# An mLSTM cell and a routed two-layer expert network on one core: weight copies on VectorE, clears on GpSimd, second-layer weights eight rows to a partition, first-layer weight columns at stride eight

## The chip, the core and the metric

The kernel runs on one core of one Trainium2 chip. The metric is the device time of one execution in microseconds, as the median over several runs; less is better. Engine names are those of the profile: PE is the matrix engine and PEld its weight loads, DVE is VectorE, ACT is ScalarE, POOL is GpSimd and SP is SyncE; a q behind a name (POOLq, SPq) is that engine's sequencer, which issues DMAs and waits.

## What is computed

Stage one is a recurrent cell over 4 batches, 8 heads, 768 steps and head width 40. Stage two sends each of the 3072 resulting rows of 320 numbers to one of 8 experts.

```python
# stage one, for t in range(768), per batch and head
m_new  = max(f + m, i);  fs = exp(f + m - m_new);  is_ = exp(i - m_new)
C = fs * C + is_ * outer(v, k);   n = fs * n + is_ * k
y = sigmoid(o) * (C @ q) / max(abs(n . q), 1)
# stage two, on x = y as 3072 rows of 320
logits = x @ w_gate                       # 320 x 8
e      = argmax(logits);  g = softmax(logits)[e]
out    = g * (relu(x @ w1[e]) @ w2[e])    # w1: 320 x 1024, w2: 1024 x 320, per expert
```

## The kernel before

**Stage one** works on 24 chunks of 128 steps, one chunk per turn `s` of a loop, all 8 heads at once. A turn loads q, k, v and the gate of chunk `s + 6` from SP's queue (L316), transposes q and k (L341), multiplies queries with keys (L359, L360) under a causal mask, carries the state (L379, L387), normalises the rows (L411 to L417) and, every second turn, computes the gate logits of two chunks (L447), the chosen experts and the places of the rows. `rank` (L506) counts with matmuls, `place` (L521) writes the slot of each row. `keep_rows` (L539, ACT) scales the rows and turns them to bf16, and `send` (L546, POOL) scatters 128 rows by slot into `x_sorted` in DRAM. Before that, `clear` writes zeros over the first 384 rows of each expert's part of `x_sorted` (L555, SP's queue, eight DMAs). PE runs a few matmuls whose product is overwritten (L354) beside the real ones, in turns 1 to 7 and in the last three.

**Stage two** is cut into groups of one or two tiles of 128 rows. I write (e, 0) for expert e's first two tiles and (e, 1) for its third tile; six "extra" tiles of whatever expert has rows left over come last. The first two groups, called `first` (0, 0) and `second` (1, 0), are written out by hand at the end of stage one. For the others a list `order` sets the sequence: (2,0), (0,1), (3,0), (1,1), (4,0), (2,1), (5,0), (3,1), (6,0), (4,1), (7,0), (5,1), (6,1), (7,1), then the six extras. The code fixes the order of all instructions by hand; no scheduler moves them. Each group does

- `turn`: transpose the rows (L233) and copy them out of PSUM on DVE (L234);
- `layer1`: 8 blocks of 128 hidden columns, three matmuls each (L245), the weights being the stationary operand; then a relu on DVE (L251) or ACT (L253);
- the `turn` of the group that follows;
- `layer2`: eight matmuls per tile (L258), a copy on ACT (L263), and a scatter of the tile to the output from POOL (L265).

The weights come from DRAM as float32 and are turned to bf16 by the DMAs themselves, all issued from POOL: two for an expert's first-layer weights (`weights_in`, L178; the first takes rows 0 to 255, the second rows 256 to 319) and one for its second layer (`weights_out`, L185). All experts' first-layer weights share one tile `w1_all` [128, 3, 8, 1024], all second-layer weights one tile `w2_all` [128, 8, 8, 320]. `weights_in(e + 2)` and `weights_out(e + 2)` stand in the code ahead of `layer1` of group (e, 0) for e = 2 to 5; those of experts 0 to 3 stand at the end of stage one. The framework puts a semaphore wait wherever an instruction reads or writes what another one wrote or read, as far as it can tell from their access patterns.

An extra tile learns its expert only from a register. For it `fetch` copies that expert's two weight matrices into buffers of their own (wx, 4 sets), with two DMAs from SP's queue (L736, L737), four groups ahead of use. `extras` (L675 to L703) is a run of small DVE instructions that works out these experts and rows, ahead of the third group of the list.

Of the kernel before, what the change touches and what calls it, by code (L numbers as in the profile page):

```python
# [19 lines left out]
def kernel(  # L20
# [41 lines left out]
    NJ = 3  # L62
# [2 lines left out]
    XU = 6  # L65
    NE = 2
    PE_ = 7
    XW = 4
    NV = 6
    NS = N + 128  # L70

# [14 lines left out]
    def pads(i):  # L86
        for t in (kp[i], qp[i]):
            nc.vector.memset(t[:, :, D:], 0.0)
        nc.vector.memset(v1[i][:, :, D:], 1.0)
# [93 lines left out]
    def weights_out(e0, n):  # L183
        e = slice(e0, e0 + n)
        nc.gpsimd.dma_start(  # L185
            w2_all[:, e].rearrange("p e a d -> p (e a) d"), moe_w2[e].rearrange("e (a p) d -> p (e a) d", p=128),
        )

    def apart(ins, group):
# [46 lines left out]
    def layer1(g, u):  # L236
        n = g["n"]
        per = 4 // n
        if u == 0:
            g["h"] = spot("h", [128, FB, n * 128], BF16)  # L240
        hp = spot("hp", [128, per, n * 128], F32)
        for i in range(per):
            fb = u * per + i
            for db in range(DB):
                nc.tensor.matmul(  # L245
                    hp[:, i, :], lhsT=g["w"][0][:, db, fb * 128 : (fb + 1) * 128], rhs=g["xT"][:, db, :],
                    start=(i == 0 and db == 0), stop=(db == DB - 1), skip_group_check=True,
                )
        dst = g["h"][:, u * per : (u + 1) * per, :]
        if u % 2 == 0:  # L250
            nc.vector.tensor_relu(dst, hp)  # L251
        else:
            nc.scalar.activation(dst, hp, AF.Relu)  # L253
# [26 lines left out]
    with tc.tile_pool(name="ring", bufs=1) as ring_pool, \  # L280
# [67 lines left out]
        def scores(s):  # L348
            d = st[s]
            kb, qb = d["kb"], d["qb"]  # L350
            sA = ps1.tile([128, PR, 128], F32, name="sA")
            sB = ps1.tile([128, PR, 128], F32, name="sB")
            for _ in range(3 if 1 <= s < 8 else 2 if s > NT - 4 else 0):
                nc.tensor.matmul(  # L354
                    sA[:].rearrange("p j t -> p (j t)"), lhsT=ident_b[:],
                    rhs=st[s - 1]["dA"][:].rearrange("p j t -> p (j t)"), start=True, stop=True,
                )
            for j in range(PR):
                nc.tensor.matmul(sA[:, j, :], lhsT=kb[0:D, j, :], rhs=qb[0:D, j, :], start=True, stop=True)  # L359
                nc.tensor.matmul(  # L360
                    sB[:, j, :], lhsT=kb[DP : DP + D, j, :], rhs=qb[DP : DP + D, j, :], start=True, stop=True,
                )
            d["dA"] = chk.tile([128, PR, 128], BF16, name="dA")
            nc.vector.tensor_tensor(d["dA"][:], sA[:], cmask[:, None, :].to_broadcast([128, PR, 128]), op=ALU.mult)
            d["dB"] = chk.tile([128, PR, 128], BF16, name="dB")
            nc.scalar.copy(d["dB"][:], sB[:])  # L366
            nc.gpsimd.affine_select(
                d["dB"][:], d["dB"][:], compare_op=ALU.is_ge, fill=0.0,
                base=0, pattern=[[0, PR], [1, 128]], channel_multiplier=-1,
            )  # L370
# [170 lines left out]
            )  # L541

        def send(t):
            if t >= NT - 7:
                nc.gpsimd.memset(tick[:], 0.0)
            ins = nc.gpsimd.indirect_dma_start(  # L546
                out=xs[:, :], out_offset=bass.IndirectOffsetOnAxis(ap=slots[:, t : t + 1], axis=0),
                in_=x_all[:, t, :], in_offset=None,
            )
            apart(ins, "rows_in")  # L550
            if t > 2 * PE_ + 1:
                tc.declare_no_dep(getattr(ins, "ins", ins), group="early", reason="later rows lie behind the early tiles")

        def clear(e):
            nc.sync.dma_start(xs[e * NS : e * NS + CAP, :].rearrange("(p j) d -> p (j d)", j=NJ), zrow[:])  # L555

        def do(f, i, *a):
            if 0 <= i < NT:
                f(i, *a)
# [10 lines left out]
            load(i)  # L570
        for i in range(1, NV):
            pads(i)
        for s in range(-3, NT):
            P, odd = (s - 4) // 2, s % 2
            last = s == NT - 1
            do(scores, s + 1)
            do(transposes, s + 2)
            if s == -3:
                masks()
            if s == -2:  # L580
                gates()
                router()
            do(values, s + 2)
            if s == NT - 3:
                weights_in(0, 1)
            if 0 <= s < E:
                nc.vector.memset(w1_all[:64, DB - 1, s, :], 0.0)
            pair = not odd and 0 <= P
            if pair:
                gate(P)  # L590
            do(states, s)
            do(load, s + 6 if s >= -1 else -1)
            if -1 <= s < 3:
                clear(2 * s + 2)
                clear(2 * s + 3)
            if pair:
                rank(P, s - 1)
            do(xtrans, s - 1)
            do(ogate, s + 2)
            do(attend, s)  # L600
            if pair:
                place(P)
                if P == PE_:
                    even_out(s - 1)
            do(keep_rows, s - 4)
            do(rows, s)
            if odd and 0 <= (s - 3) // 2:
                logits((s - 3) // 2, s - 1)
                choose((s - 3) // 2)
                count((s - 3) // 2)  # L610
            do(send, s - 5)
            late_consts(s + 1)
            if s == 20:
                for e in range(E):
                    receive(e, 0)
            if s == NT - 3:
                weights_out(0, 1)
            if s == NT - 2:
                weights_in(1, 1)
        weights_out(1, 1)  # L620
        send(NT - 5)
        gate(P0)
        rank(P0, NT - 1)
        place(P0)
        early = [dict(e=e, n=NE, k=0, si=0) for e in range(2)]
        spots.update(
            hp=[("sA", ps1), ("sB", ps1)], zp=[("tk", ps1), ("tq", ps1)], tp=[("dC", ps1)],
# [6 lines left out]
        first, second = early  # L634
        targets(0, 0)
        turn(first)
        for t in (NT - 4, NT - 3):
            keep_rows(t)
            send(t)
        for u in range(4):  # L640
            layer1(first, u)
        weights_in(2, 1)
        weights_out(2, 1)
        xtrans(NT - 1)
        targets(1, 0)
        turn(second)
        layer2(first, 0)
        logits(P0 + 1, NT)
        choose(P0 + 1)
        gate(P0 + 1)  # L650
        layer2(first, 1)
        layer1(second, 0)
        rank(P0 + 1, NT, 2 * E)
# [3 lines left out]
        for t in (NT - 2, NT - 1):  # L657
            keep_rows(t)
            send(t)
        for u in range(2, 4):  # L660
            layer1(second, u)
        weights_in(3, 1)
        weights_out(3, 1)
        layer2(second, 0)
        layer2(second, 1)

# [66 lines left out]
    def fetch(ex):  # L733
        wx1 = wk_pool.tile([128, DB, F], BF16, name="wx1", bufs=XW)
        wx2 = wk_pool.tile([128, FB, Dm], BF16, name="wx2", bufs=XW)
        nc.sync.dma_start(wx1[:], w1_all[:, :, bass.ds(ex, 1), :].rearrange("p a e b -> p a (e b)"))  # L736
        nc.sync.dma_start(wx2[:].rearrange("p a b -> p (a b)"), w2_all[:, bass.ds(ex, 1)].rearrange("p e a b -> p (e a b)"))  # L737
        return wx1, wx2

    def expert_of(x):  # L740
        return nc.sync.value_load(xe[0:1, bass.ds(x, 1)], min_val=0, max_val=E - 1)

    def row_of(x):
        return nc.sync.value_load(xb[0:1, bass.ds(x, 1)], min_val=0, max_val=E * NS - 128)
# [1 line left out]
    nc.vector.tensor_tensor(inv[:, :, NE:], posB[:], tot[:].unsqueeze(2), op=ALU.is_ge)  # L746
    for e in range(E):
        receive(e, 1)
    order = [(2, 0), (0, 1)]
    for e in range(3, E):  # L750
        order += [(e, 0), (e - 2, 1)]
    order += [(E - 2, 1), (E - 1, 1)]
    groups = [
        dict(e=e, n=(NE, NJ - NE)[k], k=k, si=(0, NE)[k], w=(w1_all[:, :, e, :], w2_all[:, e])) for e, k in order
    ] + [dict(n=1, x=x) for x in range(XU)]
# [1 line left out]
    def ready(g):  # L757
        if "x" in g:
            aim(g)
        else:  # L760
            targets(g["e"], g["k"])
        turn(g)

    ready(groups[0])
    for i, g in enumerate(groups):
        nw = g.get("e", E) + 2
        if i == 2:
            extras()
            for e_ in range(E):
                blank(e_)  # L770
        if i == 4:
            for x in range(XU):
                collect(groups[len(order) + x], row_of(x), invx[:, x : x + 1])
            exs = [expert_of(x) for x in range(XU)]
        x = i - len(order) + XW
        if 0 <= x < XU:
            groups[len(order) + x]["w"] = fetch(exs[x])
        if g.get("k") == 0 and nw < E:
            weights_in(nw, 1)
            weights_out(nw, 1)  # L780
        for u in range(FB * g["n"] // 4):
            layer1(g, u)
        if i + 1 < len(groups):
            ready(groups[i + 1])
        for j in range(g["n"]):
            layer2(g, j)
    one_order.close()
# [42 lines left out]
```

## Time and profile before

| | before |
|---|---|
| median of 3 runs (lowest, highest) | 222.78 us (222.73, 223.47) |
| the profiled execution: own time, span | 230.12 us, 228.4 us |
| PE busy, PEld busy | 200.0 us (88%), 171.6 us (75%) |
| DVE, ACT, POOL busy | 131.2, 119.0, 124.1 us |
| mean granted PE clock | 0.915 |
| weight DMAs of an expert (KB written, us to landing, median) | 512 KB 8.7; 128 KB 8.0; 640 KB 12.9 |
| copies for an extra tile | 768 KB 8.8; 640 KB 7.1 |

The page splits the span into 40 slices of 5.7 us. Stage one ends near 127 us and stage two fills the rest. "Idle before, releaser" in the groups is the time an engine stood still ahead of these instructions and what ended it. Times of single instructions are from one execution, so small differences are within what one execution shows.

### The profile page before, as it was taken

The page shows a single profiled execution, that of the slowest core. Times are in us where ns is not written, and L with a number is a line of the kernel's source. Part 1 is how long each engine was busy: PE and PEld are TensorE (multiplying, and loading weights), DVE is VectorE, ACT ScalarE, POOL GpSimd, SP SyncE. Part 2 cuts the span into 40 slices and gives each one's busy share as a digit, 9 for nine tenths or more (in the row PEclk, how much of TensorE's full clock was granted, in tenths as well). Part 3 has the DMA queues.
Part 4 walks back from the last instruction along what each step waited for, and adds up shares of the span by engine and source line. Part 5 has one row for each costly group of instructions (what it writes and reads, how often), then busy time and mean ns, then how long its engine had stood idle before and what let it go on. Part 6 is the DMA issues. An engine that isn't in the chain of part 4 may idle for free.

```text
span 228.4 us, 5745 instructions
## 1 busy us (share of the span) xinstructions
PE 200.0 (88%) x2049; PEld 171.6 (75%) x2049; DVE 131.2 (57%) x421; ACT 119.0 (52%) x275; POOL 124.1 (54%) x194
## 2 busy tenths in 40 slices
PE   2299999899999999989999699439699999999990
PEld 1168888689999999979999487327488888777770
DVE  7658878755458888888774533304834353333330
ACT  3457758744668988896943246203243433433330
POOL 5045584185166686677597855823557734333331
PEclk9999999955599999999985599958999999999999
DMA  7999999999989999898059999999999999999930
GB/s 134 174 189 167 214 199 205 203 177 192 163 151 176 169 174 188 146 193 158 17 100 284 228 232 182 174 222 234 212 216 225 216 235 311 401 399 372 392 115 0
DMA packets 122796, 46.47 MB, mean 203 GB/s; under 512 B 102474, under 2 KB 115917, under 8 KB 122768
## 3 DMA queue, kind: packets, MB, share of 16 engines
q1 hardware_dynamic: 108576, 29.50, 59.0%
q0 software_dynamic: 13728, 16.40, 36.6%
q8 instruction: 16, 0.26, 0.5%
q10 hardware_dynamic: 464, 0.21, 0.4%
q14 instruction: 12, 0.10, 0.1%
HBM read 39.38 MB, written 9.53 MB: 214 GB/s over the span
## 4 chain that ended last, share of the span: by engine, by line
PE 55%; DMA 18%; issue 7%; DVE 6%; POOL 5%; ACT 5%; SPq 3%; POOLq 0%; ACTq 0%
PE hp L447 7%; PE hp L379 7%; PE zp L258 6%; PE dC L387 6%; PE hp L245 5%; PE tk L341 5%; DMA w_all<-in_moe_w_dram 5%; PE tq L341 4%; PE xt L424 4%; DMA wx<-w_all 4%; PE sA L359 3%; POOL out_dram L265 3%; DMA x_all<-x_sorted 3%; PE sA L354 2%; DMA kq<-in_k_dram 2%
## 5 line engine op out<-in xcount | busy, mean ns | idle before, releaser
L251 DVE TENSOR_SCALAR h<-hp 128x512 bf16<-128x512 f32 x26 | 17.9, 690 | 38.7 <-PE hp L245 38.7
L265 POOL DMA_INDIRECT out_dram<-zo,s_idx x20 | 20.0, 1002 | 30.6 <-ACT zo L263 26.1
L245 PEld LDWEIGHTS <-w_all 128*128 128x128 bf16 x384 | 30.7, 100 | 6.0 <-issue 2.2
L417 POOL TENSOR_TENSOR x_sb<-x_sb,den 128x320 f32<-128x320 f32 x23 | 16.9, 733 | 27.5 <-DVE den L415 27.5
L546 POOL DMA_INDIRECT x_sorted<-x_all,slots x24 | 25.0, 1043 | 9.1 <-DMA kq<-in_q_dram 4.7
L245 PE MATMUL hp<-xT,w_all 128*128 128x128 bf16 (+1 forms) x336 | 28.9, 242 | 0.9 <-DVE xT L234 0.8
L253 ACT ACTIVATE h<-hp 128x512 bf16<-128x512 f32 x26 | 15.5, 597 | 24.5 <-PE hp L245 24.5
L258 PEld LDWEIGHTS <-h 128*128 128x128 bf16 x208 | 18.4, 101 | 12.7 <-DVE h L251 4.1
L258 PE MATMUL zp<-w_all,h 128*128 128x320 bf16 x160 | 25.8, 312 | 1.9 <-DMA out_dram<-zo,s_idx 1.9
L263 ACT COPY zo<-zp 128x320 f32<-128x320 f32 x26 | 11.1, 426 | 29.1 <-PE zp L258 27.5
L379 PE MATMUL hp<-C_sb,qT 104*128 104x82 f32 x160 | 23.3, 294 | 0.0
L379 PEld LDWEIGHTS hp<-C_sb,qT 104*128 104x128 f32 x160 | 22.3, 215 | 0.1
L341 PE MATMUL tk<-ident,kq 128*104 128x128 f32 x96 | 17.4, 310 | 5.4 <-DMA kq<-in_k_dram 5.4
L366 ACT CAST dB<-sB 128x512 bf16<-128x512 f32 x24 | 14.0, 584 | 12.9 <-PE sB L360 10.1
L426 ACT COPY xT<-xt 128x384 f32<-128x384 f32 x24 | 11.6, 483 | 16.9 <-PE xt L424 16.8
L447 PE MATMUL hp<-wg_sb,xT 128*128 128x8 f32 x144 | 20.2, 273 | 0.0
L387 PE MATMUL dC<-vA,kq 128*104 128x82 f32 x160 | 19.8, 272 | 0.0
L447 PEld LDWEIGHTS hp<-wg_sb,xT 128*128 128x128 f32 x144 | 19.5, 215 | 0.0
L329 POOL CAST vAb<-vA 128x328 bf16<-128x328 f32 x24 | 11.0, 457 | 13.5 <-DVE vA L327 13.5
L387 PEld LDWEIGHTS dC<-vA,kq 128*104 128x104 f32 x160 | 18.2, 188 | 0.0
L327 DVE TENSOR_TENSOR vA<-v,G_T 128x328 f32<-128x328 f32 x24 | 17.3, 722 | 0.7 <-DMA v<-in_v_dram 0.7
L341 PE MATMUL tq<-ident,kq 128*104 128x128 f32 x96 | 16.7, 303 | 0.2 <-DMA kq<-in_q_dram 0.2
(147 smaller groups left out, 432.4 us busy)
## 6 DMA issues: line engine op xcount, KB each, us to landing
w_all<-in_moe_w_dram POOLq DMA_DIRECT2D x8, 640.0 KB, 12.9
wx<-w_all SPq DMA_DIRECT2D x6, 768.0 KB, 8.8
w_all<-in_moe_w_dram POOLq DMA_DIRECT2D x8, 512.0 KB, 8.7
kq<-in_k_dram SPq DMA_DIRECT2D x24, 160.0 KB, 3.8
kq<-in_q_dram SPq DMA_DIRECT2D x24, 160.0 KB, 4.4
v<-in_v_dram SPq DMA_DIRECT2D x24, 160.0 KB, 4.1
o_sb<-in_o_gate_dram SPq DMA_DIRECT2D x24, 160.0 KB, 4.0
wx<-w_all SPq DMA_DIRECT2D x6, 640.0 KB, 7.1
```

The costliest lines, as they stand in the source:

```text
L245: nc.tensor.matmul(hp[:, i, :], lhsT=g["w"][0][:, db, fb * 128 : (fb + 1) * 128], rhs=g["xT"][:, db, :], start=(i == 0 and db == 0), stop= ...
L251: nc.vector.tensor_relu(dst, hp)
L253: nc.scalar.activation(dst, hp, AF.Relu)
L258: nc.tensor.matmul(zp, lhsT=g["h"][:, fb, j * 128 : (j + 1) * 128], rhs=g["w"][1][:, fb, :], start=(fb == 0), stop=(fb == FB - 1),)
L265: ins = nc.gpsimd.indirect_dma_start(out=out[:, :], out_offset=bass.IndirectOffsetOnAxis(ap=at, axis=0), in_=zo, in_offset=None, bounds_ch ...
L327: nc.vector.tensor_tensor(d["vA"][:], d["v"][:], Gb.unsqueeze(2).to_broadcast([128, H, D1]), op=ALU.mult)
L341: nc.tensor.transpose(tp[:, j, :], two(d[n], j), ident[:])
L379: nc.tensor.matmul(hp[:, 2 * j * D1 : (2 * j + 2) * D1], lhsT=d["qT"][:, j, :], rhs=st["C"][:, j].rearrange("p h d -> p (h d)"), start=(j ...
L387: nc.tensor.matmul(st["dC"][:, j], lhsT=two(d["k"], j), rhs=d["vA"][:, 2 * j : 2 * j + 2, :], start=(c == 0 and j == 0), stop=True, skip_g ...
L417: eng.tensor_tensor(x3d, x3d, den[:].unsqueeze(2).to_broadcast([128, H, D]), op=ALU.mult)
L447: nc.tensor.matmul(lg[:, i * E : (i + 1) * E], lhsT=st[t]["xT"][:, db * 128 : (db + 1) * 128], rhs=wg_sb[:, db, :], start=(fresh and i == ...
L546: ins = nc.gpsimd.indirect_dma_start(out=xs[:, :], out_offset=bass.IndirectOffsetOnAxis(ap=slots[:, t : t + 1], axis=0), in_=x_all[:, t, : ...
```

## The change

1. `weights_out` puts eight consecutive rows of w2 on a partition instead of every 128th row. Row r of the hidden layer then lies on partition r // 8, and so `layer1` takes the columns fb, fb + 8, fb + 16, ... for its block fb, a stride of eight elements.
2. `fetch` copies with two DVE instructions instead of two DMAs from SP. The register is loaded on DVE, the buffers are 3 sets instead of 4, and the call stands behind `ready` of the following group, two groups ahead of use.
3. `clear` is issued from POOL, one expert per turn in turns 0 to 7, instead of from SP, two per turn in turns -1 to 2.
4. `send` always has a one-row memset ahead of it; the first send comes in turn 9 instead of 5, after the clears, and they catch up, two in odd turns. The receives of the experts' first two tiles stand one turn earlier (19 instead of 20).
5. At the seam between the stages: three instead of two spare matmuls in the last three turns and six more ahead of `layer1` of `first`; gate, rank and place of the second last pair of chunks behind two of its four `layer1` steps; `weights_in(3)` and `weights_out(3)` ahead of `layer1(second, 2)` instead of behind `layer1(second, 3)`.
6. `order` is (2,0), (3,0), (0,1), (1,1), (4,0), (2,1), (5,0), (3,1), (4,1), (6,0), (5,1), (7,0), (6,1), (7,1).

```diff
-    XW = 4
+    XW = 3
...
-            w2_all[:, e].rearrange("p e a d -> p (e a) d"), moe_w2[e].rearrange("e (a p) d -> p (e a) d", p=128),
+            w2_all[:, e].rearrange("p e a d -> p e (a d)"), moe_w2[e].rearrange("e (p a) d -> p e (a d)", p=128),
...
-                    hp[:, i, :], lhsT=g["w"][0][:, db, fb * 128 : (fb + 1) * 128], rhs=g["xT"][:, db, :],
+                    hp[:, i, :], lhsT=g["w"][0][:, db, fb::FB], rhs=g["xT"][:, db, :],
...
-            for _ in range(3 if 1 <= s < 8 else 2 if s > NT - 4 else 0):
+            for _ in range(3 if 1 <= s < 8 or s > NT - 4 else 0):
...
-            if t >= NT - 7:
-                nc.gpsimd.memset(tick[:], 0.0)
+            nc.gpsimd.memset(tick[:], 0.0)
...
-            nc.sync.dma_start(xs[e * NS : e * NS + CAP, :].rearrange("(p j) d -> p (j d)", j=NJ), zrow[:])
+            nc.gpsimd.dma_start(xs[e * NS : e * NS + CAP, :].rearrange("(p j) d -> p (j d)", j=NJ), zrow[:])
...
-            if -1 <= s < 3:
-                clear(2 * s + 2)
-                clear(2 * s + 3)
...
-            do(send, s - 5)
+            upto = s - 4 if s >= 2 * PE_ + 4 else s - 5
+            for t in range(sent, min(upto + 1, sent + 1 + odd) if s > E else sent):
+                send(t)
+                sent = t + 1
...
+            if 0 <= s < E:
+                clear(s)
...
+        for _ in range(6):
+            j = ps1.tile([128, 512], F32, name="junk", tag="tk")
+            nc.tensor.matmul(
+                j[:], lhsT=ident_b[:], rhs=st[NT - 1]["dA"][:].rearrange("p j t -> p (j t)"), start=True, stop=True,
+            )
+        layer1(first, 0)
+        layer1(first, 1)
+        gate(P0)
+        rank(P0, NT - 1)
+        place(P0)
+        layer1(first, 2)
...
+        weights_in(3, 1)
+        weights_out(3, 1)
         for u in range(2, 4):
             layer1(second, u)
-        weights_in(3, 1)
-        weights_out(3, 1)
...
-        nc.sync.dma_start(wx1[:], w1_all[:, :, bass.ds(ex, 1), :].rearrange("p a e b -> p a (e b)"))
-        nc.sync.dma_start(wx2[:].rearrange("p a b -> p (a b)"), w2_all[:, bass.ds(ex, 1)].rearrange("p e a b -> p (e a b)"))
+        nc.vector.tensor_copy(wx1[:], w1_all[:, :, bass.ds(ex, 1), :].rearrange("p a e b -> p a (e b)"))
+        nc.vector.tensor_copy(wx2[:].rearrange("p a b -> p (a b)"), w2_all[:, bass.ds(ex, 1)].rearrange("p e a b -> p (e a b)"))
...
-    order = [(2, 0), (0, 1)]
-    for e in range(3, E):
-        order += [(e, 0), (e - 2, 1)]
-    order += [(E - 2, 1), (E - 1, 1)]
+    order = [(2, 0), (3, 0), (0, 1), (1, 1), (4, 0), (2, 1), (5, 0), (3, 1), (4, 1), (6, 0), (5, 1), (7, 0), (6, 1), (7, 1)]
...
-            exs = [expert_of(x) for x in range(XU)]
-        x = i - len(order) + XW
-        if 0 <= x < XU:
-            groups[len(order) + x]["w"] = fetch(exs[x])
...
             ready(groups[i + 1])
+        x = i - len(order) + XW - 1
+        if 0 <= x < XU:
+            groups[len(order) + x]["w"] = fetch(expert_of(x))
```

More of the change, by code (lines that the diff above doesn't have):

```diff
@@ L572 @@
             pads(i)
+        sent = 0
         for s in range(-3, NT):
@@ L604 @@
                     even_out(s - 1)
-            do(keep_rows, s - 4)
+            if s == 2 * PE_ + 4:
+                keep_rows(s - 4)
+                keep_rows(s - 3)
+            elif s != 2 * PE_ + 5:
+                do(keep_rows, s - 4)
             do(rows, s)
@@ L610 @@
                 count((s - 3) // 2)
-            do(send, s - 5)
+            upto = s - 4 if s >= 2 * PE_ + 4 else s - 5
+            for t in range(sent, min(upto + 1, sent + 1 + odd) if s > E else sent):
+                send(t)
+                sent = t + 1
+            if s == 2 * PE_ + 4:
+                send(sent)
+                sent += 1
+            if 0 <= s < E:
+                clear(s)
             late_consts(s + 1)
-            if s == 20:
+            if s == 2 * PE_ + 5:
                 for e in range(E):
@@ L620 @@
         weights_out(1, 1)
[L621 to L624, printed above, removed]
+        assert sent == NT - 4
         early = [dict(e=e, n=NE, k=0, si=0) for e in range(2)]
@@ L639 @@
             send(t)
-        for u in range(4):
-            layer1(first, u)
+        xtrans(NT - 1)
+        layer1(first, 3)
         weights_in(2, 1)
         weights_out(2, 1)
-        xtrans(NT - 1)
         targets(1, 0)
         turn(second)
-        layer2(first, 0)
         logits(P0 + 1, NT)
@@ L650 @@
         gate(P0 + 1)
+        layer2(first, 0)
         layer2(first, 1)
@@ L735, in fetch @@
         wx2 = wk_pool.tile([128, FB, Dm], BF16, name="wx2", bufs=XW)
-        nc.sync.dma_start(wx1[:], w1_all[:, :, bass.ds(ex, 1), :].rearrange("p a e b -> p a (e b)"))
-        nc.sync.dma_start(wx2[:].rearrange("p a b -> p (a b)"), w2_all[:, bass.ds(ex, 1)].rearrange("p e a b -> p (e a b)"))
+        nc.vector.tensor_copy(wx1[:], w1_all[:, :, bass.ds(ex, 1), :].rearrange("p a e b -> p a (e b)"))
+        nc.vector.tensor_copy(wx2[:].rearrange("p a b -> p (a b)"), w2_all[:, bass.ds(ex, 1)].rearrange("p e a b -> p (e a b)"))
         return wx1, wx2
     def expert_of(x):
-        return nc.sync.value_load(xe[0:1, bass.ds(x, 1)], min_val=0, max_val=E - 1)
+        return nc.vector.value_load(xe[0:1, bass.ds(x, 1)], min_val=0, max_val=E - 1)
     def row_of(x):
```

## The prediction

> **What bounds the kernel now.** I read the page's busy shares, the slices and the chain first, to find the engine and the stage.
>
> ```profile
> PE 200.0 (88%) x2049; PEld 171.6 (75%) x2049; DVE 131.2 (57%) x421; ACT 119.0 (52%) x275; POOL 124.1 (54%) x194
> PE   2299999899999999989999699439699999999990
> PEclk9999999955599999999985599958999999999999
> PE 55%; DMA 18%; issue 7%; DVE 6%; POOL 5%; ACT 5%; SPq 3%; POOLq 0%; ACTq 0%
> ```
>
> PE is the bound, near full in both stages. It dips at the seam (slices 23 to 27, 131 to 160 us), and thrice its clock is halved. The list of waits says what PE stood still for:
>
> ```profile
> PE tp L233 <- DMA x_all<-x_sorted: 5.9, 1, 5.9
> PE tk L341 <- DMA kq<-in_k_dram: 5.4, 2, 4.0
> PE zp L258 <- DMA out_dram<-zo,s_idx: 1.9, 1, 1.9
> PE hp L506 <- DVE cums L471: 1.3, 1, 1.3
> ```
>
> The 5.9 us are the rows of (0, 1), which come second in `order` but are sent late. In no line does PE wait for weights: a group asks only for its own expert's. An edit outside PE's path is thus worth nothing until it makes PE wait, and one that makes PE wait counts in full.
>
> **What the Trainium skill says.** "TensorE: Matmul & The Clock Gate", section "Part 1: The HAM clock gate (the "warmup" mystery)": an idle window of about 3.4 us halves PE's clock until it has been busy as long. The trace agrees: in the 4 us after the 5.9 us wait the clock was 0.55. "VectorE: DVE Perf Modes", "What auto-detection actually checks": a 16-bit copy at unit step gets two elements per cycle, and four only if source and destination have outer dimensions both even or equal; no copy of this kind is in the trace. "SBUF — State Buffer", "Specifications (TRN2)": lines are 16 bytes and full bandwidth wants two hits per line; a stride of eight bf16 hits each once. Against it, "TensorE: Matmul & The Clock Gate", "Weight-path perf modes — Fast Weight Load (FWL) and DoubleRow", lists packed and strided reads alike. No strided load is in the trace.
>
> **The stride, and the waits it brings.** Semaphores are placed from access patterns. I read the waits of the changed program as built. The columns fb, fb + 8, ... of one expert now count as overlapping the first weight DMA (rows 0 to 255) of any other expert that was issued earlier, though they share no element:
>
> ```
> layer1(first, 0)  waits also for w1 of expert 1
> layer1(second, 0) for expert 2      layer1(second, 2) for expert 3
> (2,0) for 4    (3,0) for 5    (4,0) for 6    (5,0) for 7
> ```
>
> Expert e + 2's DMA is issued right ahead of (e, 0), so PE waits for a prefetch. The price comes from the timeline of PE, ACT and POOL:
>
> ```profile
> 157.93 1.25 PE L258 MATMUL zp<-w_all,h 128*128 128x320 bf16 x8
> 159.02 2.98 PE L245 MATMUL hp<-xT,w_all 128*128 128x256 bf16 x24
> 159.22 0.43 ACT L263 COPY zo<-zp 128x320 f32<-128x320 f32 x1 [0.82 <-PE zp L258]
> 159.92 0.98 POOL L265 DMA_INDIRECT out_dram<-zo,s_idx  x1 [1.74 <-ACT zo L263]
> 160.87 1.38 POOL L178 DMA_DIRECT2D w_all<-in_moe_w_dram  x2
> ```
>
> PE ends `layer2` at 159.02 and goes on. The copy and the scatter come next, and the weights are issued at 160.87, 1.85 us after PE is free. In the changed kernel PE cannot go on until they land: first packets came 1.6 us after issue, 256 packets take 3.2 us (expert 1's 320 took 4.0), the receipt about 0.45: 5.3 us. With transfers ahead of them landings took 6.7 to 9.2. **Stall 1.85 + 5.3 = 7.2 us** (6 to 9), four times: **+28.8**. Each exceeds an idle window, so half clock follows: about 2.5 us lost each (one to two windows at half, 1.7 to 3.4): **+10**.
>
> `layer1(second, 2)` has expert 3's DMA moved ahead of it, behind two scatters that need the rank at L506. In the trace the rank is at 137.70, the scatters at 140.27 and 141.55, the weights at 142.52, 4.8 us after the rank; PE would be there 0.8 after it. With 6 to 8.5 us to land, 4.8 + 6 − 0.8 = 10 us, and 1.5 of half clock: **+11.5** (8 to 14). Expert 2's wait costs about **1.3**, as its issue moves ahead of the turn of `second`; expert 1's has landed: 0. Behind each stalled L245 stand all later matmuls, and so relus, copies and the next scatters: everything shifts.
>
> The load itself: loads at L245 last 100 ns (page, part 5), but overlap; a one-tile pair of load and matmul takes 56 ns (24 in 1.34 us), a two-tile one 112. At half the load bandwidth some 100 ns per load would hide under two tiles and add 44 ns in the 336 one-tile pairs: +15. I take 0 by the FWL section.
>
> **The copies on DVE.** The twelve transfers removed are hidden:
>
> ```profile
> wx<-w_all SPq DMA_DIRECT2D x6, 768.0 KB, 8.8
> ```
>
> PE never waits for wx, so removing them is worth 0. What is added lies ahead of the relu of the extras, where PE runs without gaps and DVE has this:
>
> ```profile
> 205.72 1.50 PE L245 MATMUL hp<-xT,wx 128*128 128x128 bf16 x24
> 207.06 0.33 PE L233 MATMUL tp<-ident_b,xgx 128*128 128x128 bf16 x3
> 207.39 1.28 PE L258 MATMUL zp<-wx,h 128*128 128x320 bf16 x8
> 208.51 1.50 PE L245 MATMUL hp<-xT,wx 128*128 128x128 bf16 x24
> L251 DVE TENSOR_SCALAR h<-hp 128x512 bf16<-128x512 f32 x26 | 17.9, 690 | 38.7 <-PE hp L245 38.7
> L234 DVE COPY xT<-tp 128x384 bf16<-128x384 bf16 x14 | 5.0, 356 | 0.8 <-PE tp L233 0.3
> ```
>
> An extra takes PE 208.51 − 205.72 = 2.79 us. DVE would need, per extra: first-layer copy, three runs of 1024 against a flat 3072, so two per cycle, estimated from the perf-mode page at 1.7; second-layer copy, flat 2560, four per cycle, 0.8; register load 0.3 (my choice; not in the trace on DVE), relu 0.65, xT 0.4, hand-over 0.1: 3.95. DVE becomes the bound for six extras: 6 × (3.95 − 2.79) ≈ **+6.5** (0.6 with four per cycle in both and the load hidden; 9 with one window of half clock or slower copies).
>
> **Order and seam.** (3,0) in second place hides the 5.9 us and its half clock of about 1.65: **−7.6**. The rank behind two `layer1` steps hides the 1.3 on cums: **−1.3**. Spare matmuls: +3 and +6 at 0.215 us are 1.9, of which 0.65 falls into the wait on xT; with what they may keep of the clock, **+1** (−4, if the stretch at half clock at 118 to 132 us goes, to +2.6). The 1.9 us of zp L258 are really the DVE extras ahead of a relu (158.6 to 163.3) and stay.
>
> **POOL and SP queues.** The eight clears leave SP's queue (eight issues) for POOL's, in turns 0 to 7, where POOL idles 2.4 to 3 us in two turns and about 2.15 (two issues of some 1 us) are added: 0. If that cover is gone, `rows` (L417) and the sends come late, at most +1.5. Taking them off SP could spare the loads of k that PE waits on (L341): 0 to −1.4, taken as 0. The one-row memsets (90 ns each) lie beside other work: +0.3 (inside the +1's bounds). Later sends in turns 9 on have until the receives in turn 19: 0.
>
> **Eight rows to a partition.** Expert 1's w2 alone took 4.2 us in 640-byte packets, w1's like volume 4.0; gain up to 0.3 us a transfer, off PE's path: 0 (to −2).
>
> **Sum:** 28.8 + 10 + 11.5 + 1.3 + 6.5 − 7.6 − 1.3 + 1 = **+50.2**. The profiled execution took 230.12 us, 7.3 above the median 222.78; one stretch of 17 us at half clock, at 46 to 63 us behind the k load (slices 8 to 10), is worth about that, and I take the runs shown to be without it. So 280.3 in a like profile and **273 us** as median.
>
> **Rivals.**
> *The waits find their transfers landed.* Speaks for it: before, PE met no weight wait. Against: the transfers are issued after PE is free, so nothing can have landed. Then −7.6 − 1.3 + 1 + 0.6 = −7.3: **215.5**, faster. This is the other side: with the tail hidden, the order's gain decides as soon as the seven waits together cost under 7.3 us, about one of the four stalls I price.
> *Waits free, DVE the tail's bound:* +6.5 instead of 0.6: **221.4**.
> *The strided loads are slow too:* the main case + 15: **288**; speaks for it the 16-byte line, against it the FWL section.
> *The change doesn't do what it says:* the new order cannot shorten anything if the rows' wait merely moves to another group; then +7.6 on the main case, **281**, inside its range.
>
> **How the numbers follow.** Main case 0.77 (own range 258 to 287, the term ranges combined as independent); slow loads 0.16; waits free 0.05 with the tail hidden or half hidden (0.035 well faster) and the rest spread to 240. Range 256 to 291. A measurement of this kernel tells about 0.5% (1.1 us) from no change: faster 0.04, same 0.02, slower 0.94.
>
> **What would show it.** Right: in the list of waits of the changed kernel, PE hp L245 on DMA w_all, four times near 7 us, once near 10; clock at half in the slices behind them; POOL's L178 issued inside those gaps; no L233 wait of 5.9; extras every 3.9 us with L245 waiting on DVE. DVE copies of 1.7 and 0.8 us. L245 loads still near 100 ns and one-tile pairs at 56 (slow-load rival: near 100 a pair). Wrong: L245 waits under 2 us each, or L178 issued before the preceding `layer2` ends.

## The result, and the profile after

The changed kernel takes 285.48 us in the median of 4 runs (284.93 to 287.13); the kernel before took 223.12 us in the runs beside it. The ratio is 1.2815 (95% interval 1.2743 to 1.2886): 62 us slower. 273.0 us were forecast, with 256 to 291 as the range. Here and below, ratios compare only executions outside the slower state that every kernel shows at times, while medians are over all, so the two can differ a little.

From the page of the changed kernel, the busy shares and the slices of PE and its clock (a slice is now 7.1 us):

```profile
PE 203.7 (72%) x2058; PEld 171.8 (61%) x2058; DVE 143.6 (51%) x434; ACT 118.3 (42%) x275; POOL 128.6 (45%) x219
PE   3499999999999899865407090971672999968830
PEclk9999999999999999669656777797596899999995
```

PE's busy time has hardly grown (203.7 against 200.0 us) while the span grew by 55: PE stands still. The holes lie in slices 17 to 31, counted from 0, from the seam to the group (5,0), and the clock is down there. The list of PE's waits names the reason (us in total, times, longest):

```profile
PE hp L245 <- DMA w_all<-in_moe_w_dram: 48.3, 7, 10.2
PE zp L258 <- DVE h L251: 6.4, 6, 2.3
PE tk L341 <- DMA kq<-in_k_dram: 4.4, 1, 4.4
```

The line on L245 and w_all was not in the list before. It has seven waits. The timeline of PE gives each in brackets; in order they stand in the steps `layer1(first, 0)`, `layer1(second, 0)` and `layer1(second, 2)` and at the start of the groups (2,0), (3,0), (4,0) and (5,0):

```profile
122.86 2.57 PE L245 MATMUL hp<-kq,w_all 128*128 128x256 bf16 x11 [3.04 <-DMA w_all<-in_moe_w_dram]
137.04 1.29 PE L245 MATMUL hp<-kq,w_all 128*128 128x256 bf16 x5 [5.56 <-DMA w_all<-in_moe_w_dram]
150.19 2.56 PE L245 MATMUL hp<-kq,w_all 128*128 128x256 bf16 x11 [10.17 <-DMA w_all<-in_moe_w_dram]
163.33 4.33 PE L245 MATMUL hp<-xT,w_all 128*128 128x256 bf16 x23 [6.79 <-DMA w_all<-in_moe_w_dram]
177.60 4.02 PE L245 MATMUL hp<-xT,w_all 128*128 128x256 bf16 x23 [7.33 <-DMA w_all<-in_moe_w_dram]
200.34 4.59 PE L245 MATMUL hp<-xT,w_all 128*128 128x256 bf16 x23 [8.43 <-DMA w_all<-in_moe_w_dram]
217.28 4.65 PE L245 MATMUL hp<-xT,w_all 128*128 128x256 bf16 x23 [6.99 <-DMA w_all<-in_moe_w_dram]
```

One stall seen from all its engines, ahead of (3,0), is the counterpart of the five lines that the prediction took its price from:

```profile
170.00 0.27 PE L245 MATMUL hp<-xT,w_all 128*128 128x256 bf16 x1
170.20 0.43 ACT L263 COPY zo<-zp 128x320 f32<-128x320 f32 x1 [0.66 <-PE zp L258]
171.18 1.02 POOL L265 DMA_INDIRECT out_dram<-zo,s_idx  x1 [0.30 <-issue]
172.18 1.36 POOL L178 DMA_DIRECT2D w_all<-in_moe_w_dram  x2
...
177.60 0.65 PE L245 MATMUL hp<-xT,w_all 128*128 128x256 bf16 x2 [7.33 <-DMA w_all<-in_moe_w_dram]
```

One matmul of (3,0) passes, then PE stops. Expert 5's weights are issued 2.2 us later, behind the copy and the scatter of the group before, and 5.4 us after the issue PE goes on: it waited for weights that it doesn't need for several groups.

All seven stalls begin like this one: a single matmul of the step passes, and the second one waits. Of each hidden block the first matmul reads part 0 of the expert's w1 in the tile [128, 3, 8, 1024], the second part 1. The strided columns stay within the expert's own 1024. What reaches over other experts is the DMA of rows 0 to 255: it writes parts 0 and 1 of its expert, and between these two pieces lies part 1 of every expert with a smaller number. The framework seems to take the two pieces for one stretch as soon as the read is strided. In the changed program as built, each of the seven waits hangs on the load of part 1; built with that DMA split in two, one for each part, the program has waits for its own weights alone, but this form was not timed.

### The profile page after: what moved, and what is told of

It is laid out like the page before. It is cut to its first block, busy times and chain, and to the rows that moved or that the text cites. A ratio compares the mean times of both kernels' runs of the same rounds, so it can differ in the third digit from the quotient of the medians.

```text
span 283.1 us, 5781 instructions
## 1 busy us (share of the span) xinstructions
PE 203.7 (72%) x2058; PEld 171.8 (61%) x2058; DVE 143.6 (51%) x434; ACT 118.3 (42%) x275; POOL 128.6 (45%) x219
## 3 DMA queue, kind: packets, MB, share of 16 engines
q0 software_dynamic: 7072, 18.38, 29.4%
## 5 line engine op out<-in xcount | busy, mean ns | idle before, releaser
L245 PEld LDWEIGHTS <-w_all 128*128 128x128 bf16 x384 | 39.5, 151 | 56.8 <-DMA w_all<-in_moe_w_dram 50.6
L245 PE MATMUL hp<-xT,w_all 128*128 128x128 bf16 (+1 forms) x336 | 37.4, 274 | 30.3 <-DMA w_all<-in_moe_w_dram 29.5
L245 PE MATMUL hp<-kq,w_all 128*128 128x256 bf16 x48 | 10.5, 385 | 18.8 <-DMA w_all<-in_moe_w_dram 18.8
L379 PE MATMUL hp<-C_sb,qT 104*128 104x82 f32 x160 | 20.6, 272 | 0.0
L379 PEld LDWEIGHTS hp<-C_sb,qT 104*128 104x128 f32 x160 | 19.4, 192 | 0.3
L447 PE MATMUL hp<-wg_sb,xT 128*128 128x8 f32 x144 | 17.9, 256 | 0.1
L387 PE MATMUL dC<-vA,kq 128*104 128x82 f32 x160 | 17.8, 254 | 0.0
L367 POOL TENSOR_SCALAR_AFFINE_SELECT dB<-dB 128x512 bf16<-128x512 bf16 x24 | 16.5, 689 | 1.7 <-ACT dB L366 1.5
L447 PEld LDWEIGHTS hp<-wg_sb,xT 128*128 128x128 f32 x144 | 17.1, 192 | 0.1
L364 DVE TENSOR_TENSOR dA<-sA,cmask 128x512 bf16<-128x512 f32 x24 | 16.0, 666 | 1.7 <-PE sA L359 1.7
```

Source lines behind the costliest of these rows:

```text
L245: nc.tensor.matmul(hp[:, i, :], lhsT=g["w"][0][:, db, fb::FB], rhs=g["xT"][:, db, :], start=(i == 0 and db == 0), stop=(db == DB - 1), ski ...
L367: nc.gpsimd.affine_select(d["dB"][:], d["dB"][:], compare_op=ALU.is_ge, fill=0.0, base=0, pattern=[[0, PR], [1, 128]], channel_multiplier=-1,)
L379: nc.tensor.matmul(hp[:, 2 * j * D1 : (2 * j + 2) * D1], lhsT=d["qT"][:, j, :], rhs=st["C"][:, j].rearrange("p h d -> p (h d)"), start=(j ...
L387: nc.tensor.matmul(st["dC"][:, j], lhsT=two(d["k"], j), rhs=d["vA"][:, 2 * j : 2 * j + 2, :], start=(c == 0 and j == 0), stop=True, skip_g ...
L447: nc.tensor.matmul(lg[:, i * E : (i + 1) * E], lhsT=st[t]["xT"][:, db * 128 : (db + 1) * 128], rhs=wg_sb[:, db, :], start=(fresh and i == ...
```

## The experiments

Twelve kernels ran. The ratios are to the kernel before on the same chip; chips differ, so kernels from different chips are compared by their ratios. "Expert by expert" means w1_all as [128, 8, 3, 1024], so that no expert's bytes lie between another's:

```diff
-    w1_all = big.tile([128, DB, E, F], BF16)
+    w1_all = big.tile([128, E, DB, F], BF16)
```

**The stride undone in the changed kernel.**

```diff
-                    hp[:, i, :], lhsT=g["w"][0][:, db, fb::FB], rhs=g["xT"][:, db, :],
+                    hp[:, i, :], lhsT=g["w"][0][:, db, fb * 128 : (fb + 1) * 128], rhs=g["xT"][:, db, :],
```

(and w2 back to `(a p)`.)

> The changed kernel with the weight columns read in one piece again (fb*128 to fb*128+127) and w2 back to every 128th row; everything else of the change stays. Theory (the stride brings waits for other experts' DMAs): all seven L245 waits on w_all go, 48.3 us of waiting and the half clock behind them; 220 us (216 to 226), L245 pairs back to 56 ns, the extras still paced by DVE at about 3.4 us. Rival (order, seam, clears or copies cost the time): 245 us or more, with new waits under other names.

Measured: 225.79 us (222.68 to 227.64) beside 226.13 of before (223.44 to 233.72), too few executions for a ratio. The whole loss is gone, and everything else of the change is still there. PE's L245 waits for weights are 3.2 us in four pieces, for an expert's own weights.

**The stride kept, only the waits taken away**: w1_all expert by expert, and a flat copy for the extras.

> The changed kernel with w1_all laid out expert by expert ([128, 8, 3, 1024]), stride and eight-row layout kept, and the copy of an extra's w1 thereby flat on both sides. No two experts' bytes interleave, so no wait for another expert's DMA is placed. Theory (false waits, the strided loads themselves cost little): 219 us (215 to 226), L245 pairs at about 62 ns as in the changed kernel, wx1 copies 0.9 us instead of 1.74. Rival (the strided read itself is slow or disturbs): 240 us or more.

Measured: 228.0 us, ratio 1.0119 (1.0052 to 1.0186). With the strided reads still in place, 57 us of span have gone (283.1 to 226.2), 2.6 of them by the flat copy (PE's wait for DVE's relu fell from 6.4 to 3.8). Of the 48.3 us on L245 this is left:

```profile
PE hp L245 <- DMA w_all<-in_moe_w_dram: 2.4, 2, 2.2
```

So the waits are the loss, and the strided read is not. Two smaller expectations showed as well: the flat copy takes 0.96 us, and the one-tile pairs 62 ns. By its ratio it stayed some 7 us over the expectation; the end of the run and the dearer loads, both measured below, make up most of that.

**The stride alone in the kernel before** (the two edits above the other way round, and the eight rows of w2).

> The kernel before with only the stride of eight and the eight-row layout of w2. Theory: the waits alone make the loss: L245 waits on w_all before first, second, (2,0), (3,0), (4,0), (5,0), (2,0) for two prefetches at once, about 12 us but hiding the 5.9 us wait for rows; 48 us of waits and half clock in all: 271 us (258 to 285). Rival (the moved prefetch of expert 3 and the new order are needed for it): under 245 us.

Measured: 271.85 us, ratio 1.2068 (1.1977 to 1.2159). The waits in order are 4.4, 1.1, 13.5, 7.4, 7.6 and 7.9 us, together 41.8. These two edits make most of the loss by themselves; neither the moved prefetch nor the new order is needed.

**The prefetch issued one `layer2` earlier**, which shortens each stall and leaves the waits where they are.

```diff
-        if g.get("k") == 0 and nw < E:
-            weights_in(nw, 1)
-            weights_out(nw, 1)
         for u in range(FB * g["n"] // 4):
             layer1(g, u)
+        if i + 1 < len(groups) and groups[i + 1].get("k") == 0 and groups[i + 1]["e"] + 2 < E:
+            weights_in(groups[i + 1]["e"] + 2, 1)
+            weights_out(groups[i + 1]["e"] + 2, 1)
```

(and expert 4's likewise ahead of `layer2` of `second`.)

> The changed kernel, but weights_in(e + 2) and weights_out(e + 2) issued one layer2 earlier, ahead of the output scatters of the group before (e, 0); the waits stay. Theory (a stall is issue delay after layer2 plus landing): the stalls before (2,0) and (3,0) fall by about 4 us each (layer2 of two tiles 2.2 and 1.9 of copy and scatter), before (4,0) and (5,0) by about 3: 29.5 falls to about 15, with less half clock: 267 us (260 to 275). Rival (landing is set by bandwidth or by the queue, not by the time of issue): 283 us or more.

Measured: 271.36 us, ratio 1.1985 (1.186 to 1.211). The four stalls in the timeline of PE of this kernel:

```profile
157.94 2.73 PE L245 MATMUL hp<-xT,w_all 128*128 128x256 bf16 x23 [1.05 <-DMA w_all<-in_moe_w_dram]
167.45 4.40 PE L245 MATMUL hp<-xT,w_all 128*128 128x256 bf16 x23 [4.15 <-DMA w_all<-in_moe_w_dram]
188.54 4.24 PE L245 MATMUL hp<-xT,w_all 128*128 128x256 bf16 x23 [4.85 <-DMA w_all<-in_moe_w_dram]
203.92 5.07 PE L245 MATMUL hp<-xT,w_all 128*128 128x256 bf16 x23 [5.75 <-DMA w_all<-in_moe_w_dram]
```

They sum to 15.8 us, against 29.5; about 15 was expected. A stall is the delay of the issue plus the time to land.

**The layout as such**: the control for the runs that use it.

> The kernel before with nothing but w1_all laid out expert by expert: the control for the runs that use this layout to be rid of the waits. If the layout costs nothing, the ratio to before is 1.00 (0.995 to 1.005), and the 1.055 of the kernel before with stride, eight rows and this layout is all due to stride and eight rows. If the layout itself costs (longer pieces in the extras' transfers, other landings at the seam), this run lies at 1.01 to 1.03.

Measured: ratio 0.9992 (0.9958 to 1.0026). It costs nothing. Its profile, of span 220.7 us, also serves below as the base, since the profile before had 32 us of PE's work at half clock and this one has 7.

**Neither stride nor eight rows, with flat copies.**

> The changed kernel with w1_all expert by expert, weight columns in one piece and w2 back to every 128th row: no stride, no eight-row layout, both copies of an extra flat. Against the same kernel with the stride and the eight rows (228.0 us, span 226.2) it should lose the dearer loads (62 against 56 ns in 336 one-tile pairs, 2 us) and the long end (10.2 us from the last scatter to the end, 4.2 in kernels without the stride, 6 us): 220 us (217 to 224). Rival (the long end comes with the copies on DVE or the expert-major layout): 226 us.

Measured: 222.1 us, ratio 0.9947 (0.9913 to 0.998). The span of its profile is 220.1 us, 6.1 less than with stride and eight rows, but on another chip; by the ratios the gain is 1.7 per cent, some 4 us, where 8 were expected.

**Eight rows without the stride, and two rows to a piece.**

```diff
-            w2_all[:, e].rearrange("p e a d -> p e (a d)"), moe_w2[e].rearrange("e (p a) d -> p e (a d)", p=128),
+            w2_all[:, e].rearrange("p e (a b) d -> p e a (b d)", b=2), moe_w2[e].rearrange("e (a p b) d -> p e a (b d)", p=128, b=2),
```

(The second of these runs; the first leaves the line of the change.)

> As the changed kernel with w1_all expert by expert, eight rows of w2 to a partition kept, but weight columns in one piece; the hidden rows so meet the wrong rows of w2, which changes the output and none of the work. It parts the two halves of the edit for the end of the run. If POOL's closing drain follows the layout of w2 (fewer and larger packets on its queue): the drain stays at 7.1 us, 226 us. If it follows the stride: drain 2.2 us, 220 us.

> As the kernel with straight columns and eight rows of w2 to a partition, but two rows to a piece, four pieces a partition; again w1's columns meet the wrong rows, which changes the output and none of the work. POOL's queue then moves some 10,150 packets, between 7,072 and 14,240. If the closing drain falls with the number of packets: about 4.7 us. If it follows the size of a packet past some bound: 7.1 or 2.3 us.

Measured: ratio 1.0155 (1.0076 to 1.0233) for the first; the second was run once, 233.17 us on a slower chip. What tells them apart is the drain that POOL runs at the end. In the profile's lines on the program's last line, the numbers are the shortest, median and longest in ns; first the kernel with w2 by every 128th row, then eight rows, then two:

```profile
L837 POOLq DRAIN  x3: 46/109/2367, 216.9 to 219.8; - x3
```

```profile
L837 POOLq DRAIN  x3: 46/109/7093, 215.7 to 223.3; - x3
```

```profile
L837 POOLq DRAIN  x3: 46/109/7093, 223.5 to 231.2; - x3
```

The long drain follows w2's layout and not the stride. It doesn't follow the number of packets on POOL's queue either, 7,072 in the second kernel and 10,144 in the third. It was long with two rows to a piece and with eight; why is open.

**Copies on DVE alone, in the kernel before.**

```diff
-        nc.sync.dma_start(wx1[:], w1_all[:, :, bass.ds(ex, 1), :].rearrange("p a e b -> p a (e b)"))
+        nc.vector.tensor_copy(wx1[:], w1_all[:, :, bass.ds(ex, 1), :].rearrange("p a e b -> p a (e b)"))
```

(likewise wx2; register, sets and place as in the change.)

> The kernel before with the extras' weights copied by DVE, three buffers, two groups ahead; nothing else. Theory (DVE is the bound of the extras: copies of 1.75 and 0.82 us, a period of 3.4 against PE's 2.8, and 2.5 us ahead of the first): 4 to 6 us slower than before, about 2 per cent. Rival (the copies hide behind PE, and the transfers removed had slowed the end): within 1 us of before or faster.

Measured: 230.73 us, ratio 1.0304 (1.0226 to 1.0382), about 6.8 us, somewhat over the 4 to 6 expected. In the tail PE waits 5.6 us, for a relu (2.5) or for the small DVE operation that aims the output (3.1); in the control it waits 0.2 us there.

**The order alone, in the kernel before.**

```diff
-    order = [(2, 0), (0, 1)]
...
+    order = [(2, 0), (3, 0), (0, 1), (1, 1), (4, 0), (2, 1), (5, 0), (3, 1), (4, 1), (6, 0), (5, 1), (7, 0), (6, 1), (7, 1)]
```

> The kernel before with the new order of groups alone, (3,0) ahead of (0,1). Prediction: the 5.9 us wait for the rows of (0,1) and its 1.65 us of half clock are hidden: 7.6 us faster, ratio 0.966. Rival (expert 3's weights or rows arrive as late, and the wait takes another name): within 2 us of before.

Measured: 222.19 us, ratio 0.9914 (0.9874 to 0.9954). This missed: 0.9 per cent instead of 3.4. PE's waits in this kernel, beside those of before (its profiled execution took 222.67 us, its fastest 219.0):

```profile
PE zp L258 <- DVE h L251: 2.9, 2, 2.7
PE hp L245 <- DMA w_all<-in_moe_w_dram: 2.4, 1, 2.4
...
PE zp L258 <- DMA w_all<-in_moe_w_dram: 2.0, 2, 1.3
```

The wait for rows is gone, and 4.4 us of waiting for an expert's own weights, first and second layer, has come; 3.7 us of it stand in the moved group (3,0), which needs weights that aren't there yet.

**Order, seam, clears and sends alone**: all copies by SP again, no stride, no eight rows.

> The changed kernel with w1_all expert by expert, straight columns, old rows of w2, and the extras' weights fetched by SP's transfers again, four buffers, four groups ahead: of the change only order, seam, clears and sends are left. Theory: the waits of PE on relu and copies in the tail (5.4 us with flat copies) fall to the 2 us that belong to the DVE extras, the rest stays: 219 us (216 to 221), a ratio near 0.98. Rival (the tail is held by something else, or the transfers collide with the last weights): 222 us as with the flat copies.

Measured: ratio 0.9862 (0.9808 to 0.9915), 228.21 against 232.57 us on that chip. This is the fastest against before, though its interval touches that of the order alone, and it beats both kernels: the change without its weight layouts and without DVE's copies is worth 1.4 per cent.

**Stride and eight rows without the waits, in the kernel before.**

> The kernel before with stride and eight-row layout, but w1_all expert by expert, so that no wait for another expert is placed. Theory (the loss of the stride is the waits; beside them it costs 2 us of loads and 5 us of POOL's closing drain): 7 us slower than before, ratio 1.03. Rival (the strided read disturbs more than that, in the seam or with the transfers): 240 us or more.

Measured: ratio 1.0546 (1.0465 to 1.0626), 1.8 times the loss expected. Of some 12.5 us the drain is 4.3 (6.44 us against 2.11 in the control) and the one-tile loads some 2. In this profile PE also waits 4.1 us for ACT's relu, 0.7 to 1.0 us a time in four one-tile groups and an extra, which the control doesn't show; but the kernel above, on the same slower chip and without the stride, has 2.3 us of that too. No profile of the control is from that chip, so how much of the rest is the stride's stays open.

## Why the prediction was right, and where its sum was off

The mechanism and the sign were right, and the likeliest case came about. The time alone doesn't say so: 285 us lies nearer to the rival with slow loads (288) than to the main case (273). It is the waits and the loads in the trace that tell them apart. The forecast sum was +50.2 us; measured are +62.4, in both the medians and the spans (283.1 against 220.7 of the control). The terms can be read off the two profiles:

| term | forecast | measured |
|---|---|---|
| four stalls, (2,0) to (5,0) | 28.8 | 29.5 |
| expert 3's wait, in `second` | 10 | 10.2 |
| expert 2's wait | 1.3 | 5.6 |
| expert 1's wait | 0 | 3.0 |
| half clock, more than in the control | 11.5 less 1.65 | 9.8 |
| DVE in the tail and the extras | 6.5 | 4.7 |
| loads at stride eight | 0 | 2.0 |
| rows' wait and cums' wait gone | −5.9 and −1.3 | −7.4 and −1.5 |
| spare matmuls (counted, nine at 0.215) | 1 | 1.9 |
| from the last scatter to the end | not in the sum | 6.2 |

The measured column adds up to 64.0. It differs from 62.4 by 1.6 because the terms touch each other and small waits are left out.

**The stalls** held to 3 per cent: 1.85 us of delay and 5.3 of landing were forecast, and the stall shown has 2.2 and 5.4. The delay is longer where the group before has two tiles, as its second scatter follows the first on POOL. Landings took 5.2 to 6.7 us, and the longest makes the longest of the four stalls, 8.4 us ahead of (4,0).

**Half clock** after the four stalls was priced at 2.5 us each. The clock's stretches in the windows of the changed kernel (length, then PE busy with its count) are:

```profile
159.85:166.68 6.83, 3.35 (x16) 2.64 (x17) 0.69 (x1) 0.60 (x1) 0.00 (x0) 0.50 0.92 175
173.51:180.33 6.82, 2.73 (x13) 2.18 (x14) 0.69 (x1) 0.13 (x1) 0.61 (x2) 0.50 1.02 183
193.99:204.23 10.24, 3.89 (x19) 3.07 (x20) 0.70 (x2) 0.60 (x1) 1.45 (x3) 0.50 0.98 181
214.47:221.29 6.82, 4.01 (x19) 3.15 (x20) 0.81 (x2) 0.60 (x1) 0.00 (x0) 0.50 0.94 182
```

The clock was at half for 6.8 or 10.2 us, but PE stood still in much of that. Half of its busy time there is lost: 1.7, 1.4, 1.9 and 2.0 us. This agrees with the Trainium skill, "TensorE: Matmul & The Clock Gate", Part 1, on windows of about 3.4 us: the stretches are two or three of them. In one thing the trace differs from the page: the window ahead needn't be idle. In the 3.4 us before the stretch that begins at 115.48, PE was busy for 2.6 us and stood still for at most 0.8 at a time. Half clock during a wait costs nothing, which the forecast's 2.5 neglected; all stretches together cost 13.4 us, 9.8 more than in the control.

**Expert 1's and 2's waits are the mis-sized step.** "Expert 1's has landed: 0" was a misreading of the profile before, which has the wait in reach. The second line is the time from the issue of the first of these two DMAs to its landing:

```profile
123.58 1.30 POOL L178 DMA_DIRECT2D w_all<-in_moe_w_dram  x2
DMA to landing us min/median/max: 8.4/8.4/8.4
128.90 4.22 PE L245 MATMUL hp<-kq,w_all 128*128 128x256 bf16 x24 [0.65 <-DVE kq L234]
```

The weights land at 132.0, 3.1 us after PE starts on `layer1` of `first`. In the changed kernel they are issued at 114.59, land 8.2 us later, and PE comes at 119.40: 3.0 us of waiting.

For expert 2 the forecast took the issue to move ahead of the turn of `second`. It stands ahead of it in the code of both kernels. What moves is the rank of the chunks before, now behind two steps of `layer1(first)`, and with it the two sends that stand ahead of the weights on POOL:

```profile
127.89 1.03 POOL L545 DMA_INDIRECT x_sorted<-x_all,slots  x1 [10.02 <-ACT x_all L539]
...
129.22 1.00 POOL L545 DMA_INDIRECT x_sorted<-x_all,slots  x1 [0.21 <-issue]
130.21 1.36 POOL L178 DMA_DIRECT2D w_all<-in_moe_w_dram  x2
131.21 0.27 PE L245 MATMUL hp<-kq,w_all 128*128 128x256 bf16 x1
```

POOL idles 10 us for rows that ACT scales only after the rank. PE comes 1.0 us after the issue, against 5.7 before (131.38 and 137.05), and the landing takes 6.8. With the stride alone and the old seam this wait is 1.1 us. The first stall doesn't lengthen the second: with the stride undone, the rank, the issue and PE's arrival are at 120.26, 125.22 and 126.20, here at 125.22, 130.21 and 131.21, all 5 us later.

**The tail.** The copies came out as forecast from the Trainium skill's rule on outer dimensions ("VectorE: DVE Perf Modes", "What auto-detection actually checks"), and this case's runs agree with it:

```profile
250.07 1.74 DVE L752 COPY wx<-w_all 128x3072 bf16 x1
251.73 0.82 DVE L753 COPY wx<-w_all 128x2560 bf16 x1
252.47 0.69 DVE L251 TENSOR_SCALAR h<-hp 128x512 bf16<-128x512 f32 x1
```

3072 elements from three runs take 1.74 us, 2560 flat ones 0.82; flat on both sides, the same 3072 take 0.96. The period is 3.42 us, not 3.95; 0.3 us of the difference is the register load, which doesn't show between DVE's instructions. The last extras thus cost less than forecast. In the kernel before alone, the copies cost 6.8 us.

**The strided loads** took 146 ns in the median at L245 instead of 98; their means are in the pages of the changed kernel and of the kernel before:

```profile
L245 PEld LDWEIGHTS <-w_all 128*128 128x128 bf16 x384 | 39.5, 151 | 56.8 <-DMA w_all<-in_moe_w_dram 50.6
L245 PEld LDWEIGHTS <-w_all 128*128 128x128 bf16 x384 | 30.7, 100 | 6.0 <-issue 2.2
```

A one-tile `layer1` took 1.48 us instead of 1.34. The rival that priced them at 15 us falls; so does my 0. Neither of the two sections of the Trainium skill that the prediction set against each other gives this price.

**The order** was right in the sum for the wrong reason. Its own gain is 0.9 per cent. In the changed kernel the weights that it waits for are already counted among the false waits, so the rows' wait vanished whole.

**The end** was the term I did not have: from the end of the last scatter to the end of the span 10.2 us pass, in the control 4.0, and POOL's drain lasts 7.09 us and 2.11; the other 1.2 us were not followed up. Nothing in the page's groups or the chain of before shows a drain, as sequencer instructions aren't counted as busy. The rival with waits that find their transfers landed fell with the first line of the waits.

## What to carry to other kernels

A framework that places waits by access pattern may tie a strided read of a shared tile to transfers that share no element with it. Before changing a stride or a layout in a tile that is filled while it's read, list the waits that the built program gains, and lay the tile out so that what one transfer writes lies in one stretch, with nothing of others in between: here one swap of two dimensions in the tile was worth over 50 us. Price a wait for a prefetch as the delay of its issue behind PE's last work plus its landing; and when work is moved ahead, ask whether its own data arrives earlier too.

## What the runs showed of the hardware

POOL's closing drain took 2.1 to 2.4 us with w2 moved row by row and 6.4 to 7.1 us when a piece held two or eight rows (7,072 and 10,144 packets on its queue gave the same 7,093 ns); it lies on the end of every run. Loads of 128 bf16 columns at a stride of eight last half as long again, 146 against 98 ns, and cost 6 ns of 56 in a pair with a 128-column matmul and nothing with a 256-column one.
